# Moving sums of the first product into DRAM transfers, regrouping its border rounds and reordering the DFT's first steps in a spectral-plus-MoE kernel

## The chip, the cores and the metric

The kernel runs on one NeuronCore of one Trainium2 chip. The metric is the device time of one execution in microseconds (us). Five engines work side by side, each on its own queue in order: TensorE (PE, with its weight loads PEld), VectorE (DVE), ScalarE (ACT), GpSimd (POOL) and SyncE (SP), which here only issues DMA transfers. Sixteen DMA engines move the data.

## The reference

A token mixer of two branches on the same x, 2048 tokens by 512, all in float32:

```python
a = x @ dft_hid_re.T ;  b = x @ dft_hid_im.T             # DFT along the 512
A = dft_seq_re @ a - dft_seq_im @ b                        # real part of the DFT along the 2048 tokens
gates = softmax(x @ w_gate)                                # all 8 experts are taken (K = 8)
B = sum(gates[:, e] * (silu(x @ w1[e]) @ w2[e]) for e in range(8))   # hidden size 1376 per expert
g = sigmoid((x * gate_w).sum(-1))
out = g * A + (1 - g) * B
```

## The kernel before, in words

Every float32 product is made of three matmuls on operands split in two: `mm` (L348) issues high by high (L349), high by low (L352), low by high (L353). A split is two instructions: ACT copies the operand to the rounded high part (`act`, L346), and DVE or POOL subtracts it from the operand for the low part (`vt`, L343; `pt`, L340). Block products are further cut by a Strassen-like scheme with seven (2x2 blocks) or twenty (3x2x2) products, so operands are sums of blocks, made on DVE and POOL, and results are sums of products.

The program has four stages on the one core.

1. The DFT along the tokens (from the start to about 322 us) in eight phases, the list `phases` at L740: X phases use the forms 1, 2 and 5, Y phases 6, 3, 7 and 4. Each phase runs over k = 0..7. For one k, `plan_left_x` (L473) loads the four 256-wide blocks of x (`xraw`, "xr" in the rows, 512 KB), splits blocks 0 and 1 (tile "xl" from "xr"), sums blocks 2 and 3 on DVE (`s1`, tile "xq") and splits that sum (`hi`, tile "xl" from "xq"); `plan_right` (L534) loads 512 KB of the DFT matrix ("ca") and 256 KB ("cd"), takes a difference on DVE into "cd" and splits both (tiles "c12..h", "c12..l", and "c" from "cd"). `dft` (L633) issues the 18 matmuls of one k: forms 1 and 2 first, 5 last. In the first phase k = 0 and 1 are done by `dft_0` (L619), and before it `warm` (L624) issues WARM = 10 matmuls on a constant tile. In the tile names c12003l the digits are phase and k: 00 then 3.
2. The DFT along the 512 (`plan_y`, L884), four groups, to about 409 us. Beside it the twenty forms of x (`XFORM`, L76) for the next stage are made: each is one block of x transposed, or a sum or difference of two. `raw_block` (L925) loads the raw blocks, DVE adds (L986, L989, L1014, L1017), and each form is split on ACT and DVE (L997, L1020).
3. The first product of the experts (silu(x w1)), 29 rounds ("laps"), about 27 us each, to about 1195 us. A round takes three chunks of 128 hidden rows; `chunk_rows` (L44) lists them. Each expert has ten full chunks and 96 rows over; the overs of all experts make six mixed chunks. Three chunks of one expert make a pure round; what is left makes mixed rounds. `plan_round` (L1055) plans one: sums of w1 blocks on POOL (L1097), splits on ACT and POOL (L1110, L1112), 20 products, the combining sums on DVE (L1182), silu on ACT (L1198), and a multiplication by the gate of the chunk's expert on DVE (L1208). `gate` (L1037) loads that gate row spread over 128 partitions, 256 KB, and keeps it in a buffer for a following round that uses it.
4. The second product (w2), to the end.

The order of the work: in stage 1 every step is an event with a time (`ev`, L332) and the events are sorted by it; ACT, DVE, POOL and PE keep this order, and the plain loads and stores on SP are placed by the framework. From stage 2 on, a planner (`Plan.run`, L158) simulates the engines with fixed costs, gives out buffers, and the order it finds is written out. An SP transfer waits until the eighth before it on SP has landed, since eight semaphores go round.

## Time and profile before

| what | value |
|---|---|
| device time, median of 3 runs (lowest, highest) | 2019.68 us (2019.68, 2019.91) |
| the profiled execution: its own time | 2020.08 us |
| the profiled execution: span from first to last instruction | 2018.3 us |
| busy share of PE, DVE, ACT, POOL | 99%, 82%, 51%, 43% |
| matmuls | 8836 |
| moved by DMA | 475.20 MB |

The span and the 1.8 us around it make the profiled execution's own time, 0.4 us above the median. Times in the views are counted from the start of the span. An engine's idle time costs something only where PE waits for it, since PE is busy nearly throughout.

### The profile page before, as it was taken

To read this page: it belongs to the slowest core of one execution; us is meant where nothing else is said; L and a number is where in the kernel's file an instruction comes from. 1 tells how busy PE (TensorE), PEld (TensorE's weight loads), DVE (VectorE), ACT (ScalarE), POOL (GpSimd) and SP (SyncE) were. 2 spreads that over 40 slices of the span, in tenths; PEclk is the share of its full clock that TensorE was granted. 3 is DMA by queue.
4 is the path that set the end of the run, shared out by engine and by line. 5 is a ranking of instruction groups with operands and counts; after the bars stand their busy time and mean duration, and the time that the engine had idled before them with its cause. 6 is when DMAs were issued, how large, how long until landed. Compare 5 with 4: busy or idle time off the path is not lost. (4 is left out here: it accounts for less than half of the span.)

```text
span 2018.3 us, 26838 instructions
## 1 busy us (share of the span) xinstructions
PE 2006.9 (99%) x8836; PEld 1655.3 (82%) x8836; DVE 1659.0 (82%) x1929; ACT 1030.1 (51%) x1440; POOL 861.9 (43%) x829
## 2 busy tenths in 40 slices
PE   9999999999999999999999999999999999999999
PEld 7887888888888888888878888888888888888887
DVE  8998996887878887887778786687778888899875
ACT  6544453455555555555555565544445444445442
POOL 0000000188889888889798830000002221235330
PEclk9999999999999999999999999999999999999999
DMA  8676696545565546454645599899889988999991
GB/s 317 214 254 237 221 311 214 190 148 183 175 201 172 185 157 213 166 190 166 221 152 178 178 317 368 298 333 287 268 265 286 293 269 262 279 279 331 303 291 45
DMA packets 205236, 475.20 MB, mean 235 GB/s; under 512 B 22788, under 2 KB 37508, under 8 KB 205096
## 3 DMA queue, kind: packets, MB, share of 16 engines
q1 hardware_dynamic: 192280, 450.15, 64.9%
q0 software_dynamic: 12672, 23.07, 6.9%
q8 instruction: 69, 1.13, 0.2%
q14 instruction: 71, 0.58, 0.1%
q10 hardware_dynamic: 144, 0.26, 0.1%
HBM read 366.36 MB, written 107.03 MB: 235 GB/s over the span
## 5 line engine op out<-in xcount | busy, mean ns | idle before, releaser
L1198 ACT ACTIVATE psp<-psp 128x512 f32<-128x512 f32 x280 | 160.3, 582 | 208.5 <-DVE psp L1182 141.8
L1182 DVE TENSOR_TENSOR psp<-psp,tc 128x512 f32<-128x512 f32 x79 | 55.3, 699 | 33.9 <-PE psp L353 27.9
L1260 ACT ACTIVATE tc<-psp 128x512 f32<-128x512 f32 x88 | 52.4, 597 | 42.7 <-PE psp L353 32.9
L1097 POOL TENSOR_TENSOR tc<-ras 128x256 f32<-128x256 f32 x27 | 20.0, 739 | 121.9 <-DMA ras<-w_dram 120.4
L1427 POOL DMA_DIRECT2D xfx1n<-w_dram x11 | 9.9, 963 | 132.3 <-DVE xf211n L1484 94.8
L1260 ACT ACTIVATE tg<-psp 128x512 f32<-128x512 f32 x67 | 40.0, 598 | 35.4 <-PE psp L353 27.3
L1182 DVE TENSOR_TENSOR psp<-psp,tg 128x512 f32<-128x512 f32 x52 | 36.3, 699 | 21.8 <-PE psp L353 17.8
L340 POOL TENSOR_TENSOR c73011l<-cb,c73011h 128x1024 fp32r<-128x1024 f32 x1 | 2.4, 2412 | 116.8 <-ACT c73011h L346 116.8
L1112 POOL TENSOR_TENSOR wfs1nn<-tc,wfs1nn 128x512 fp32r<-128x512 f32 x32 | 42.0, 1313 | 15.4 <-ACT wfs1nn L1110 8.9
L1208 DVE TENSOR_TENSOR tc<-psp,tc 128x512 f32<-128x512 f32 x62 | 42.5, 685 | 5.2 <-ACT psp L1198 4.2
L1097 POOL TENSOR_TENSOR tc<-tc,ras 128x256 f32<-128x256 f32 x54 | 43.1, 797 | 4.2 <-DVE xfx13n L997 1.8
L1112 POOL TENSOR_TENSOR wfs3n<-tc,wfs3n 128x512 fp32r<-128x512 f32 x29 | 38.4, 1326 | 10.9 <-ACT wfs3n L1110 10.9
L1112 POOL TENSOR_TENSOR wfs2n<-tc,wfs2n 128x512 fp32r<-128x512 f32 x29 | 39.0, 1344 | 8.2 <-ACT wfs2n L1110 8.1
L346 ACT ACTIVATE c<-cd 128x512 fp32r<-128x512 f32 x32 | 20.2, 633 | 38.7 <-DVE cd L343 38.7
L1260 ACT ACTIVATE tw<-psp 128x512 f32<-128x512 f32 x41 | 24.5, 597 | 30.3 <-PE psp L353 23.3
L1182 DVE TENSOR_TENSOR psp<-psp,tw 128x512 f32<-128x512 f32 x37 | 25.9, 699 | 16.4 <-PE psp L353 14.4
L1112 POOL TENSOR_TENSOR wfs0n<-tc,wfs0n 128x512 fp32r<-128x512 f32 x26 | 35.3, 1356 | 7.8 <-ACT wfs0n L1110 7.4
L349 PE MATMUL psp<-xfx,wfs0n 128*128 128x512 f32 x94 | 36.6, 389 | 0.0
L353 PE MATMUL psp<-xfx,wfs0n 128*128 128x512 f32 x94 | 36.6, 389 | 0.0
L340 POOL TENSOR_TENSOR c12111l<-ca,c12111h 128x1024 fp32r<-128x1024 f32 x1 | 2.6, 2602 | 78.4 <-PE u L353 78.4
L1112 POOL TENSOR_TENSOR wfs0n<-tg,wfs0n 128x512 fp32r<-128x512 f32 x24 | 32.1, 1339 | 7.4 <-ACT wfs0n L1110 7.4
L1112 POOL TENSOR_TENSOR wfs3n<-tg,wfs3n 128x512 fp32r<-128x512 f32 x24 | 33.0, 1373 | 3.4 <-ACT wfs3n L1110 3.3
(3474 smaller groups left out, 7980.9 us busy)
## 6 DMA issues: line engine op xcount, KB each, us to landing
hd<-tc SPq DMA_DIRECT2D x161, 256.0 KB, 2.3
ca<-cT_dram SPq DMA_DIRECT2D x63, 512.0 KB, 5.4
hd<-tg SPq DMA_DIRECT2D x108, 256.0 KB, 2.5
hd<-tw SPq DMA_DIRECT2D x75, 256.0 KB, 2.3
cb<-cT_dram SPq DMA_DIRECT2D x32, 512.0 KB, 5.3
ras<-w_dram SPq DMA_DIRECT2D x29, 512.0 KB, 4.2
xfx12n<-hd SPq DMA_DIRECT2D x27, 512.0 KB, 5.3
ras1n<-hd SPq DMA_DIRECT2D x26, 512.0 KB, 5.4
```

The source lines that it names most:

```text
L340: pin(nc.gpsimd.tensor_tensor(*a))
L346: pin(nc.scalar.activation(dst, src, f, **kw))
L349: ins = nc.tensor.matmul(ps, lh, rh, start=start, stop=False, skip_group_check=True)
L353: nc.tensor.matmul(ps, ll, rh, start=False, stop=stop, skip_group_check=True)
L1097: pin(ins.tensor_tensor(low(b, j), src(x), src(y), o))
L1112: lambda: pin(nc.gpsimd.tensor_tensor(r(w)[:, 1, :], f(b), f(w)[:, 0, :], sub)), [oh] + deps, [b, w],
L1182: q = op("DVE", V, due, lambda: pin(nc.vector.tensor_tensor(f(dst), f(a[0]), f(b_[0]), o)), [a[1], b_[1]] + list(deps), [dst, a[0], b_[0]] ...
L1198: os = op("ACT", A, due, lambda: pin(nc.scalar.activation(f(dst), f(src_), AF.Silu, scale=sign)), [o0], [dst, src_])
L1208: oh = op("DVE", V, due + 1.2, lambda: pin(nc.vector.tensor_tensor(f(hb), f(dst), f(gb), OP.mult)), [os, og], [hb, dst, gb], lock=dst.ring ...
L1260: o = op("ACT", AP_, after(x), lambda: pin(nc.scalar.activation(f(b), f(bank[x[0]]), AF.Copy)), [prod[x]], [b, bank[x[0]]])
L1427: return op("POOL", 0.9, due, lambda: pin(nc.gpsimd.dma_start(f(src_)[:, j, :], block(key), accum_op=add, max_dma_last_dim=4096)), deps, [ ...
```

## The change

- The first matmuls: WARM goes from 10 to 17.
- The first phase of the DFT: for k = 4..7 the sum of blocks 2 and 3 of x is no longer made on DVE from the loaded x. SP loads block 2 a second time into a tile of its own, and a DMA issued by POOL adds block 3 onto it in SBUF. And for every k from 2 on (before: k = 2 alone) the low part "c12..l" is placed at s - 3.4, ahead of the difference "cd".
- The forms of x: twelve sums of two blocks, named xa to xl, are made in DRAM: SP copies one block to a DRAM tile `xs`, and a DMA issued by POOL adds the other. They are scheduled in the fourth phase of the DFT. Twelve forms are then one raw block; where the sum carries a minus sign, the sign is put into the split (ACT's scale, and a scalar_tensor_tensor on DVE). Five forms stay differences on DVE, and some forms change sign, with add and subtract exchanged in the sums of w1 blocks and the sign of one silu.
- The rounds: the mixed rounds take one mixed chunk and the last full chunk of two neighbouring experts, and stand between these two, after rounds 3, 9, 15 and 21 of the pure ones, instead of three leftover chunks in a row of the list after every second expert. The number of rounds and of products is the same.

```diff
-WARM = 10
+WARM = 17
...
-    pure = [[tuple(e * FULL + 3 * i + j for j in range(3)) for i in range(FULL // 3)] for e in range(E)]
-    rest = [e * FULL + FULL - 1 for e in range(E)] + list(range(E * FULL, NCHUNK))
-    mixed = [tuple(rest[3 * i:3 * i + 3]) for i in range(len(rest) // 3)]
     out = []
     for e in range(E):
-        out += pure[e]
-        if e % 2:
-            out.append(mixed[e // 2])
-    return out + [tuple(rest[-2:])]
+        out += [tuple(e * FULL + 3 * i + j for j in range(3)) for i in range(FULL // 3)]
+        if e % 2 == 0:
+            out.append((E * FULL + e // 2, e * FULL + FULL - 1, (e + 1) * FULL + FULL - 1))
+    return out + [(NCHUNK - 2, NCHUNK - 1)]
...
+XFORM = {16: "-21", 6: "+xa", 7: "+13", 13: "+14", 9: "+22-13", 3: "+22", 0: "+21-14", 10: "+xb",
...
+XSUM_AT = (13.0, 8.0)
...
+        def plus(j):
+            if j == 2:
+                v["q"] = xp.tile([P, 256], F32, tag="x", name=f"xq{k}_0")
+                nc.sync.dma_start(v["q"], x[k][:, j, :])
+            else:
+                pin(nc.gpsimd.dma_start(v["q"], x[k][:, j, :], accum_op=add, max_dma_last_dim=4096))
...
-        ev(s5 - 3.3, s1)
+        if k < 4:
+            ev(s5 - 3.3, s1)
+        else:
+            ev(s - 12.5, plus, 2)
+            ev(s - 8.5, plus, 3)
...
+    def x_sum(n, k, blk):
+        d, t = int(blk[0]) - 1, int(blk[1]) - 1
+        src_ = xT[2 * d:2 * d + 2, :, t * GT:(t + 1) * GT]
+        if k == 0:
+            nc.sync.dma_start(xs[n], src_)
+        else:
+            pin(nc.gpsimd.dma_start(xs[n], src_, accum_op=add, max_dma_last_dim=4096))
...
-                plan_right(pr, c, ph, k, s - 14, s - 2.9, r, lo=s - 3.4 if k == 2 else None)
+                plan_right(pr, c, ph, k, s - 14, s - 2.9, r, lo=s - 3.4)
...
+        if (pr, c, ph) == (0, 1, "Y"):
+            for n, blocks in enumerate(XSUM.values()):
+                for k, blk in enumerate(blocks):
+                    ev(T + XSUM_AT[0] * n + XSUM_AT[1] * k, x_sum, n, k, blk)
...
+    def second(dst, src, hi, neg):
+
+        if neg:
+            return nc.vector.scalar_tensor_tensor(dst, src, -1.0, hi, OP.mult, sub)
+        return nc.vector.tensor_tensor(dst, src, hi, sub)
```

The order of three queues at the places that matter. SP in the first phase, before: the loads of x ("xr") and of the DFT matrix for k = 5, 6, 7 (the digit after xr, the last digit after ca00 and cd00).

```order
L542 DMA ca005_249<-cT_dram 128x1024
L544 DMA cd005_251<-cT_dram 128x512
L481 DMA xr5_246<-x_dram 128x1024
L542 DMA ca006_288<-cT_dram 128x1024
L481 DMA xr6_285<-x_dram 128x1024
L544 DMA cd006_290<-cT_dram 128x512
L542 DMA ca007_328<-cT_dram 128x1024
L481 DMA xr7_325<-x_dram 128x1024
L544 DMA cd007_330<-cT_dram 128x512
```

SP at the same place, changed:

```order
L557 DMA ca005_259<-cT_dram 128x1024
L501 DMA xq4_0_230<-x_dram 128x256
L559 DMA cd005_261<-cT_dram 128x512
L485 DMA xr5_256<-x_dram 128x1024
L501 DMA xq5_0_272<-x_dram 128x256
L557 DMA ca006_301<-cT_dram 128x1024
L485 DMA xr6_298<-x_dram 128x1024
L559 DMA cd006_303<-cT_dram 128x512
L501 DMA xq6_0_313<-x_dram 128x256
L557 DMA ca007_342<-cT_dram 128x1024
L485 DMA xr7_339<-x_dram 128x1024
L559 DMA cd007_344<-cT_dram 128x512
```

Four loads of 128 KB ("xq") have come in between; the fourth, xq7_0, stands right behind the last row shown. DVE at the end of the first phase, before ("c12010l" is the first low part that the second phase needs, "c5007" and "xl5_6" from "xq7" are the parts of form 5 at k = 7):

```order
L343 TENSOR_TENSOR c12007l_408<-ca007_328,c12007h_407 128x1024
L343 TENSOR_TENSOR cd010_367<-cd010_367,ca010_365 128x512
L343 TENSOR_TENSOR c12010l_416<-ca010_365,c12010h_415 128x1024
L343 TENSOR_TENSOR c5007_418<-cd007_330,c5007_418 128x512
L343 TENSOR_TENSOR xl5_6_375<-xq7_0_410,xl5_6_375 128x256
```

DVE there, changed:

```order
L347 TENSOR_TENSOR c12007l_422<-ca007_342,c12007h_421 128x1024
L347 TENSOR_TENSOR cd007_344<-cd007_344,ca007_342 128x512
L347 TENSOR_TENSOR c5007_430<-cd007_344,c5007_430 128x512
L347 TENSOR_TENSOR cd010_382<-cd010_382,ca010_380 128x512
L347 TENSOR_TENSOR c12010l_428<-ca010_380,c12010h_427 128x1024
L347 TENSOR_TENSOR xl5_6_390<-xq7_0_353,xl5_6_390 128x256
```

The difference cd007 now follows c12007l, and c5007 stands ahead of c12010l. ACT's order is as before in this phase: high part of the sum xq7, then c12010h, then c5007. POOL from its start to the sixth phase, changed; before, the rows of L503 and L761 are not there:

```order
L643 MEMSET one_92 128x128
L503 DMA xq4_0_230<-x_dram 128x256
L503 DMA xq5_0_272<-x_dram 128x256
L503 DMA xq6_0_313<-x_dram 128x256
L503 DMA xq7_0_353<-x_dram 128x256
L344 ISA
L344 TENSOR_TENSOR c73011l_1135<-cb011_1088,c73011h_1134 128x1024
L344 TENSOR_TENSOR c64011l_1141<-ca011_1086,c64011h_1140 128x1024
L761 DMA xs_83<-xT_dram 256x512 x3
L344 TENSOR_TENSOR c12101l_1475<-ca101_1435,c12101h_1474 128x1024
L344 TENSOR_TENSOR c5101_1484<-cd101_1437,c5101_1484 128x512
L761 DMA xs_83<-xT_dram 256x512 x7
```

POOL holds its adding transfers in its own order: three stand behind the low part c64011l of the fourth phase and seven behind c5101 of the fifth.

More of the change, by code (lines that the diff above doesn't have):

```diff
@@ L991, in fnet_moe_kernel @@
+                dep.append(op("DVE", V2 if k is None else V, xdue[m] - 2.6, go,
                               oa + ob, [s_, a_, b_], lock=True, rel=xdue[m] - XDUE[5]))
-        last = None
+        last, neg = None, sa == "-"
         for k, (s_,) in each((src,)):
-            oh = op("ACT", A2 if k is None else A, xdue[m] - 1.4, lambda h=h, s_=s_, k=k: pin(
-                nc.scalar.activation(r(h) if k is None else r(h)[:, k, :], part(s_, k), AF.Copy)),
+            oh = op("ACT", A2 if k is None else A, xdue[m] - 1.4, lambda h=h, s_=s_, k=k, neg=neg: pin(
+                nc.scalar.activation(r(h) if k is None else r(h)[:, k, :], part(s_, k), AF.Copy, scale=-1.0 if neg else 1.0)),
@@ L996, in fnet_moe_kernel @@
                 dep, [h, s_], rel=xdue[m] - XDUE[5])
-            last = op("DVE", V2 if k is None else V, xdue[m], lambda l=l, h=h, s_=s_, k=k: pin(nc.vector.tensor_tensor(
-                r(l) if k is None else r(l)[:, k, :], part(s_, k), part(h, k), sub)), [oh, last], [l, h, s_], lock=True)
+            last = op("DVE", V2 if k is None else V, xdue[m], lambda l=l, h=h, s_=s_, k=k, neg=neg: pin(second(
+                r(l) if k is None else r(l)[:, k, :], part(s_, k), part(h, k), neg)), [oh, last], [l, h, s_], lock=True)
@@ L1011, in x_half @@
-        (qa, oa), (qb, ob) = halves
-        if sa == "-":
-            def go():
-                pin(nc.vector.scalar_tensor_tensor(f(qa), f(qa), -1.0, f(qb), OP.mult, sub))
-        else:
-            def go():
-                pin(nc.vector.tensor_tensor(f(qa), f(qa), f(qb), add if sb == "+" else sub))
-        os = op("DVE", V + 0.2 * (sa == "-"), xdue[m] - 2.6, go, [oa, ob], [qa, qb], lock=True)
-        oh = op("ACT", A, xdue[m] - 1.4, lambda: pin(nc.scalar.activation(r(h)[:, k, :], f(qa), AF.Copy)), [os], [h, qa])
@@ L1020, in x_half @@
-        return op("DVE", V, xdue[m], lambda: pin(nc.vector.tensor_tensor(r(l)[:, k, :], f(qa), f(h)[:, k, :], sub)), [oh],
+            halves.append((q, load(xdue[m] - 6, lambda q=q, blk=blk: nc.sync.dma_start(f(q), x_block(blk)[k]), MB, bufs=[q],
+                                   rel=xdue[m] - 10)))
+        qa, os = halves[0]
+        if len(terms) == 2:
+            (_, oa), (qb, ob) = halves
+            os = op("DVE", V, xdue[m] - 2.6, lambda: pin(nc.vector.tensor_tensor(f(qa), f(qa), f(qb), sub)), [oa, ob],
+                    [qa, qb], lock=True)
@@ L1021, in x_half @@
+        neg = terms[0][0] == "-"
+        oh = op("ACT", A, xdue[m] - 1.4, lambda: pin(nc.scalar.activation(
+            r(h)[:, k, :], f(qa), AF.Copy, scale=-1.0 if neg else 1.0)), [os], [h, qa])
+        return op("DVE", V, xdue[m], lambda: pin(second(r(l)[:, k, :], f(qa), f(h)[:, k, :], neg)), [oh],
                   [l, h, qa], lock=True)
@@ L1134, in plan_round @@
             s5 = sums(b5, [(1, "12", "22", add)], d4 - 4.0, [])
-            s4 = sums(b4, [(0, (b5, 1), "11", add)], d4 - 3.2, s5)
+            s4 = sums(b4, [(0, "11", (b5, 1), sub)], d4 - 3.2, s5)
             split(b4, (0, (10, 14)), d4, s4 + [u4])
@@ L1140, in plan_round @@
             u6 = unit(b6, 0, "21", d6)
-            s6 = sums(b6, [(1, "11", "32", sub)], d6 - 3.2, [])
+            s6 = sums(b6, [(1, "11", "32", add)], d6 - 3.2, [])
             split(b6, ((17, 12), 18), d6, s6 + [u6])
@@ L1144, in plan_round @@
             s7 = sums(b7, [(0, "12", "32", add), (1, "21", "31", add)], d7 - 4.2, [])
[L1145 removed]
+            s9 = sums(b9, [(1, (b7, 1), "12", sub), (1, (b9, 1), "22", sub)], d7 - 2.6, s7)
             split(b7, (15, 1), d7, s7 + s9)
@@ L1195, in finish_out @@
             row, j = divmod(i, 4)
+            sign = -sign if j == 1 else sign
             src_, o0 = val[name]
```

47 lines of the change are left out of this document (22 added, 25 removed).

## The prediction

> **What bounds the kernel now.** I read the page first, then the busy times in stretches of 50 us, then what PE waited for, then the stretches with the time line. The page's first part:
>
> ```profile
> PE 2006.9 (99%) x8836; PEld 1655.3 (82%) x8836; DVE 1659.0 (82%) x1929; ACT 1030.1 (51%) x1440; POOL 861.9 (43%) x829
> ```
>
> The matmuls stay the same 8836 but for seven more warming calls, so only PE's losses can be won. Busy time, with the number of instructions in brackets, by stretch:
>
> ```profile
> core 0: us, PE busy (x) PEld busy (x) DVE busy (x) ACT busy (x) POOL busy (x), PEclk, DMA share, GB/s
> 0.00:50.00 50.00, 46.45 (x199) 38.45 (x200) 41.84 (x69) 32.57 (x51) 0.56 (x6) 0.97 0.85 316
> 50.00:100.00 50.00, 50.00 (x222) 41.40 (x222) 49.43 (x75) 26.66 (x35) 0.00 (x0) 1.00 0.60 215
> 100.00:150.00 50.00, 49.60 (x220) 40.79 (x219) 47.91 (x62) 21.23 (x21) 4.78 (x2) 1.00 0.77 253
> ...
> 400.00:450.00 50.00, 48.97 (x216) 40.15 (x215) 41.50 (x52) 28.39 (x49) 41.02 (x37) 1.00 0.48 160
> ...
> 750.00:800.00 50.00, 49.44 (x217) 40.35 (x217) 39.76 (x57) 28.37 (x51) 42.38 (x44) 1.00 0.59 200
> ...
> 1000.00:1050.00 50.00, 48.93 (x215) 39.72 (x214) 40.16 (x56) 26.97 (x49) 43.35 (x44) 1.00 0.52 173
> ```
>
> A full stretch holds 222 matmuls, so one takes 50 / 222 = 0.225 us. The three stretches of the first product lack 6 + 5 + 7 = 18 matmuls: 18 x 0.225 = 4.1 us. The stretch from 100 lacks two, 0.5 us. The rest of the loss is in the first 50 us. What PE waited for:
>
> ```profile
> PE u L619 <- ACT c L346: 2.1, 1, 2.1
> ...
> PE psp L349 <- ACT tc L1260: 1.0, 1, 1.0
> PE psp L353 <- POOL wfs2n L1112: 0.7, 1, 0.7
> PE psp L349 <- ACT tg L1260: 0.6, 1, 0.6
> PE u L349 <- DVE s L343: 0.4, 1, 0.4
> PE psp L349 <- ACT tw L1260: 0.4, 1, 0.4
> PE u L352 <- DVE c12003l L343: 0.3, 1, 0.3
> ```
>
> So everything that this change could remove is about 4.1 us in the first product and some 2 to 3 us at the start. A gain or a loss of 0.2% is 4.0 us, about what a measurement of this kernel can tell from no change.
>
> **The change, part by part: the warming.** The start, by the clock that PE was granted (third number from the end):
>
> ```profile
> 4.07:7.49 3.42, 1.29 (x10) 1.06 (x9) 0.87 (x2) 1.53 (x3) 0.00 (x0) 1.00 0.95 354
> 7.49:10.90 3.41, 3.41 (x9) 2.64 (x8) 3.04 (x6) 1.82 (x4) 0.00 (x0) 0.50 1.04 395
> 14.30:36.00 21.70, 21.43 (x95) 17.41 (x95) 20.94 (x35) 14.91 (x24) 0.00 (x0) 1.00 1.03 403
> ```
>
> And the time line there (start, duration; the bracket is the idle time and its releaser):
>
> ```profile
> 1.15 3.88 PE L631 MATMUL warm<-one 128*128 128x128 f32 x20 [1.15 <-POOL one L628]
> 7.16 10.07 PE L619 MATMUL u<-c,xl 128*128 128x512 f32 x36 [2.13 <-ACT c L346]
> 15.12 1.23 DVE L343 TENSOR_TENSOR c12002l<-ca,c12002h 128x1024 fp32r<-128x1024 f32 x1
> 17.30 0.39 PE L352 MATMUL u<-c12002l,xl 128*128 128x512 f32 x1
> 20.53 1.22 DVE L343 TENSOR_TENSOR c12003l<-ca,c12003h 128x1024 fp32r<-128x1024 f32 x1
> ```
>
> PE was busy 1.29 of 3.42 us, and in the next 3.41 us it had half its clock. The 36 first matmuls took 10.07 us instead of 36 x 0.225 = 8.1: 1.9 us. The 20 warming matmuls (two for a call) took 3.88 us, so 14 more take 14 x 0.19 = 2.7 at most, ending at 7.7 instead of 5.03; at the full clock about half of that, so they end near 6.4, ahead of 7.16. I take full clock from then on; the ends are 0.5 us later and 1.9 us earlier. But c12002l is done at 15.12 + 1.23 = 16.35 and was used at 17.30, so at most 0.95 us of it is won before DVE is late. c12003l goes ahead of two DVE steps and keeps about that for k = 3. With DVE waiting for ACT's part of cd right behind, I carry 0.8 us into k = 4.
>
> **The sum on DMA, k = 4 to 7.** It takes 0.43 us of DVE away four times, for which PE did not wait. It adds a load of 128 KB and an adding transfer behind it. What waits for the adding transfer is ACT's high part (xl from xq), and behind that, in ACT's order, everything for the next k. The end of the first phase before:
>
> ```profile
> 22.51 0.33 SPq L544 DMA_DIRECT2D cd<-cT_dram  x1
> ...
> 34.04 0.43 DVE L343 TENSOR_TENSOR xq<-xr 128x256 f32<-128x256 f32 x1
> ...
> 34.50 0.42 ACT L346 ACTIVATE xl<-xq 128x256 fp32r<-128x256 f32 x1 [0.82 <-DVE xq L343]
> 34.82 1.05 ACT L346 ACTIVATE c12010h<-ca 128x1024 fp32r<-128x1024 f32 x1
> ...
> 35.78 0.61 ACT L346 ACTIVATE c<-cd 128x512 fp32r<-128x512 f32 x1
> 36.11 0.70 DVE L343 TENSOR_TENSOR cd<-cd,ca 128x512 f32<-128x512 f32 x1
> 36.71 1.23 DVE L343 TENSOR_TENSOR c12010l<-ca,c12010h 128x1024 fp32r<-128x1024 f32 x1
> ...
> 42.34 0.39 PE L352 MATMUL u<-c12010l,xl 128*128 128x512 f32 x1
> ```
>
> The transfers: one load alone in its window, and of the adding ones that the second product has, the whole queue and the fastest and the slowest kind (KB, then the median time to landing):
>
> ```profile
> cd<-cT_dram SPq DMA_DIRECT2D x1, 256.0 KB, 9.5
> q0 software_dynamic: 12672, 23.07, 6.9%
> xfx1n<-w_dram POOLq DMA_DIRECT2D x11, 256.0 KB, 7.5
> ...
> wfs3nn<-w_dram POOLq DMA_DIRECT2D x3, 256.0 KB, 5.2
> ```
>
> The DMA engines are full from 7.49 to 36 us (share 1.03, 403 GB/s), so every byte put in moves what follows. cd for k = 7, the last load ahead of xq7, landed at 22.51 + 9.5 = 32.0. The four xq loads add 4 x 131 KB / 403 GB/s = 1.3 us. An adding transfer of 256 KB held all engines for 0.069 x 2018.3 / 88 = 1.58 us (88 = 23.07 MB by 256 KB), so one of 128 KB holds them for 0.8, and three lie ahead: 2.4 us. xq7 lands near 35.7. The adding transfer then takes between 5.2 - 0.8 = 4.4 and 7.5 - 0.8 = 6.7 us; the engines are fuller here than there but the transfer is small, so I take 5.0, and down to 3.6 if its latency shrinks with its size. The sum lands at 40.7, where ACT had it at 34.50.
>
> From there in the changed order: ACT's parts of xq7, c12010h and c5007 start 0.32 and 0.96 us apart and the last takes 0.61, with its wait 2.0 us; then on DVE c5007 and cd010, 0.6 us each from start to start like cd above, and c12010l 1.23: about 4.5 us. c12010l is ready at 45.2 and was used at 42.34: **+2.9 us**. The ends: landing of xq7 0.7 earlier with 3.6 gives 35.0 + 3.6 + 4.5 - 42.3 = +0.8; 0.5 later with 6.7 gives +5.1. It swallows what the warming won, since PE waits here for a landing. The same chain at k = 4 (xq4 follows the load of ca for k = 5) is late by less, so the last one counts. Nothing behind gives it back: PE runs at its own pace to 400 us.
>
> The Trainium skill, page "DMA: Bandwidth & Descriptors", section "Anatomy of one DMA — SWDGE (gpsimd) path", gives such a transfer 2.0 us plus its bytes at 436 GB/s: an estimate of 2.3 us for 128 KB, by which this term would be +0.2. The rows above, 5.2 to 7.5 us for 256 KB against its 2.6, speak against that in a loaded kernel.
>
> **The sums in DRAM.** Twelve copies and twelve adding transfers of 512 KB, spread by SP's order over about 40 to 260 us. An adding one holds the engines for 3.2 us, a copy 1.5 (450.15 MB in 64.9% of the span):
>
> ```profile
> q1 hardware_dynamic: 192280, 450.15, 64.9%
> ```
>
> That is 12 x 4.7 = 56 us in 220 us, of which the shares of 0.60 to 0.77 leave 50 to 88 us free. Three adding ones stand in a row on POOL behind c64011l, in the stretch from 100 us, and seven behind c5101; each waits for its copy, and c12101l and c12111l are queued behind them, but the copies stand far ahead on SP. In the waits above PE waits for no load. I take 0, and up to +1.5 if a pile-up there outlasts the loads' lead. On the other side DVE loses some fifteen additions between 330 and 430 us, and eight low parts become scalar_tensor_tensor, which costs no more (min/median/max in ns):
>
> ```profile
> L986 DVE SCALAR_TENSOR_TENSOR xf201n<-wfs,xfw x1: 1221/1221/1221, 357.4 to 357.4; 128x1024 f32<-128x1024 f32 x1
> L989 DVE TENSOR_TENSOR wfs<-xfx,wfs x1: 1220/1220/1220, 359.6 to 359.6; 128x1024 f32<-128x1024 f32 x1
> ```
>
> DVE is busy 41.50 of 50 us there, and PE's one wait in that stretch, 1.0 us, was for ACT: I take 0, and at best that wait with its refilling, -1.3.
>
> **The rounds.** Gate loads fall by twelve of 256 KB in SP's order; every mixed round still needs three gates at once, two of which its neighbours use as well. The wait in the stretch from 750 us stands at the first product of round 14, right behind the mixed round 13 (counted from 0):
>
> ```profile
> 791.19 0.50 PE L349 MATMUL psp<-xf16n,wfs0n 128*128 128x512 f32 x1 [0.56 <-ACT tg L1260]
> ```
>
> The two of the stretch from 1000 us stand in round 22, a pure one behind a pure one. The new plan has another order everywhere, and such waits come from small differences between plan and chip. Of the 4.1 us I take 1.0 as won; the ends are -3.0 and +1.5. A changed sign costs nothing.
>
> **The sum.** +2.9 + 0 + 0 - 1.0 = +1.9 against the profiled execution's own 2020.08 us: 2022.0; against the median, which stands 0.4 us lower, 2019.68 + 1.9 = **2021.6 us**. That is +0.1%, no change that a measurement can tell. Its own range, with the ends added in part: -0.5 to +4.0, or 2019.2 to 2023.7.
>
> **The rivals.**
> Faster: the adding transfers hide. For it speaks the skill's 2.3 us; against it the rows. Then the start wins 0.8 and the laps 1.0: 2017.9 us. Below -4 us it gets only if also nearly all laps' waits go: -0.8 - 3.6 gives 2015.3.
> Slower: the landings come late and the clock closes as well. Once an adding transfer takes more than about 6.5 us, the chain costs 5 us, and PE idles 1 to 2 us within some 3.4 us, as it did before 7.49, after which it had half its clock for 3.41 us; while PE waits anyway, about 1 of those 1.7 us counts. +5.0 + 1.0 - 0.5 gives 2025.2. Against it: 1.3 to 2 us of idle are fewer than the 2.13 of the start. The skill's page "TensorE: Matmul & The Clock Gate", section "Part 1: The HAM clock gate", has the gate close after one idle window of about 3.4 us; the trace shows the half clock after a window 38% busy.
> Worse laps: the new order brings more waits than it takes, 3 us, beside +2.9: 2025.6 us.
>
> **How the numbers follow.** The forecast has 0.58, nearly all of it within 0.2%, 0.04 slower. The hidden transfers have 0.20, of which 0.08 is faster by over 0.2%. Late landings have 0.15 and worse laps 0.07, nearly all slower by over 0.2%, 0.20 together. So faster 0.08, same 0.68, slower 0.24. The range runs from 2016.8, leaving out the best of the laps, to 2025.2.
>
> **What would show it.** In the changed profile: the 36 first matmuls in about 8.2 us with the clock at 1.00; ACT waiting for a DMA ahead of xl from xq four times, near 28, 32, 36 and 40 us; the first low product of phase two near 45 us instead of 42.34; DFT stretches from 50 to 320 us full with 222; fewer than 18 matmuls missing in the first product. If xl from xq does not wait, or phase two starts before 42 us, the step on the adding transfer is wrong. If the 50 us stretches of the DFT lack matmuls, the step on the DRAM sums is.

## The result, and the profile after

| | time, us | against before |
|---|---|---|
| before | 2019.80 (2019.68 to 2020.24) | |
| changed | 2043.47 (2040.53 to 2047.44, four runs) | ratio 1.0118, 95% interval 1.0103 to 1.0133 |

The change costs 23.7 us. The forecast was +1.9, with a range that ended at 2025.2. The changed kernel also scatters more, 7 us over its four runs, where the kernel before stays within 0.6. Its profiled execution took 2047.44 us with a span of 2045.7. That is the slowest of the four, 4.0 us above their median, so the losses read from its trace are larger than the 23.7 by about as much.

The first part of its page, and the queue on which the adding transfers of POOL run (packets, MB, share of the engines):

```profile
PE 2018.8 (99%) x8850; PEld 1660.5 (81%) x8850; DVE 1643.1 (80%) x1907; ACT 1027.8 (50%) x1439; POOL 877.7 (43%) x845
...
q0 software_dynamic: 16512, 29.89, 9.0%
```

DVE did become less busy, by 16 us, and no time was won with it. The stretches of 50 us show where the matmuls are missing (a full one holds 222):

```profile
0.00:50.00 50.00, 45.23 (x190) 36.96 (x191) 34.11 (x54) 28.05 (x45) 4.18 (x10) 0.97 0.82 294
...
100.00:150.00 50.00, 48.09 (x206) 39.32 (x205) 47.50 (x63) 21.09 (x22) 6.63 (x5) 0.97 0.79 241
150.00:200.00 50.00, 46.34 (x197) 36.27 (x196) 38.86 (x47) 19.35 (x23) 7.36 (x6) 0.97 0.92 292
...
250.00:300.00 50.00, 41.84 (x178) 34.14 (x177) 34.81 (x45) 17.95 (x27) 8.63 (x9) 0.93 0.88 275
300.00:350.00 50.00, 48.96 (x212) 39.28 (x211) 46.89 (x57) 26.01 (x29) 0.00 (x0) 1.00 0.75 256
```

Everything is lost in the DFT. Stretches of the DFT that lack matmuls were the prediction's sign that its step on the DRAM sums is wrong; those from 150 us on show it. (What is missing between 100 and 150 us lies around a wait for DVE at 125.79 us and belongs to the start.) What PE waited for, the four longest:

```profile
PE u L356 <- DVE c12116l L347: 8.2, 1, 8.2
PE u L353 <- ACT c L350: 2.7, 1, 2.7
PE lt L401 <- ACT xs_2h L350: 2.5, 1, 2.5
PE u L353 <- DVE s L347: 1.9, 1, 1.9
```

In the first three the engines named, DVE and ACT, were not the cause: they waited for a transfer themselves (ahead of the third, ACT stood 7.33 us for a load "ca"). In the fourth, DVE was busy: 3.36 of the 3.43 us around it. The second wait, on the time line, with POOL's adding transfer for k = 4, ACT behind it, and PE:

```profile
22.99 1.01 POOL L503 DMA_DIRECT2D xq<-x_dram  x1 [21.89 <-DMA xq<-x_dram]
...
29.73 0.42 ACT L350 ACTIVATE xl<-xq 128x256 fp32r<-128x256 f32 x1 [5.89 <-DMA xq<-x_dram]
30.05 0.61 ACT L350 ACTIVATE c<-cd 128x512 fp32r<-128x512 f32 x1
...
30.71 0.50 PE L353 MATMUL u<-c,xl 128*128 128x512 f32 x1 [2.70 <-ACT c L350]
```

The sum for k = 4 landed 6.7 us after POOL had issued it, and ACT stood for 5.89 us. The longest wait, near 290 us:

```profile
281.15 1.60 SPq L559 DMA_DIRECT2D cd<-cT_dram  x2
...
285.26 0.39 PE L353 MATMUL u<-c12116h,xl 128*128 128x512 f32 x1
291.33 0.69 DVE L347 TENSOR_TENSOR cd<-cd,ca 128x512 f32<-128x512 f32 x1 [12.32 <-DMA cd<-cT_dram]
...
293.81 0.79 PE L356 MATMUL u<-c12116l,xl 128*128 128x512 f32 x1 [8.16 <-DVE c12116l L347]
```

SP issued the load of cd116 (the "cd" of the seventh phase at k = 6) at 281.15 us and it came 10 us later. DVE could not begin the difference before, and the low part c12116l stands behind that difference. The order of SP says why the load was issued so late. Before:

```
L542 DMA ca113_2168<-cT_dram 128x1024
L544 DMA cd116_2287<-cT_dram 128x512
L542 DMA ca114_2206<-cT_dram 128x1024
```

On the time line before, SP issued it at 233.28 us, 22.7 us ahead of ca116. In the changed kernel cd116 stands behind ca116 and seven more transfers: ca117, four stores of ud and two loads of wd. The framework has placed the loads anew; run 7 below shows that the copies on SP alone do not bring cd116 there.

The clock paid again behind these waits. The granted clock (third number from the end) in a window of 3.4 us around the wait near 193 us, and in the next one:

```profile
191.70:195.09 3.39, 1.08 (x4) 0.50 (x5) 2.73 (x4) 2.19 (x3) 0.00 (x0) 1.00 1.09 305
195.09:198.50 3.41, 3.41 (x9) 2.63 (x8) 3.27 (x5) 0.76 (x2) 0.00 (x0) 0.50 1.07 339
```

PE was busy a third of the first window and got half its clock in the second, with 9 matmuls instead of 15. Six matmuls are 6 x 0.225 = 1.4 us beside the wait itself. It happened four times in the DFT.

To follow a loss through the program I compare when the first matmul of a step starts in two time lines. The row "before" has its start in us; every other row has how much later that kernel is there. Each row is one execution; those of the changed kernel and of run 14 stand 4.0 us above and 3.8 us below the median of their runs, the others within 3 us of it. The steps are k = 5 of the first phase (c12005), the first one of the second and of the fourth phase (c12010, c64010), k = 4 of the fifth (c12104), k = 7 of the seventh (c12117), k = 1 of the eighth (c64111), the first product, and the last matmul.

| kernel | c12005 | c12010 | c64010 | c12104 | c12117 | c64111 | first product | end |
|---|---|---|---|---|---|---|---|---|
| before | 29.9 | 42.1 | 118.8 | 182.5 | 274.6 | 284.1 | 409.2 | 2013.1 |
| changed | 3.9 | 5.2 | 7.0 | 12.7 | 24.9 | 27.2 | 28.4 | 27.7 |
| 1 neither | -0.7 | 3.2 | 4.2 | 4.2 | 4.2 | 4.2 | 5.1 | 7.2 |
| 2 start adds | 3.5 | 5.1 | 6.7 | 6.7 | 6.7 | 6.7 | 6.7 | 6.8 |
| 3 DRAM sums | -0.5 | 2.8 | 4.9 | 13.2 | 28.5 | 30.6 | 31.9 | 31.2 |
| 4 copies on POOL | -0.8 | 2.7 | 4.1 | 5.0 | 23.6 | 25.2 | 27.0 | 26.9 |
| 5 low order | -0.5 | 2.7 | 4.4 | 4.4 | 4.4 | 4.4 | 4.4 | 3.9 |
| 6 warming, rounds | -0.1 | -0.1 | -0.1 | 0.0 | 0.0 | 0.0 | 0.0 | 2.4 |
| 7 no DRAM adds | -0.6 | 2.7 | 5.0 | 6.8 | 6.8 | 8.7 | 10.0 | 9.4 |
| 8 cd order | -0.5 | 2.8 | 4.8 | 12.1 | 17.1 | 24.6 | 25.8 | 26.9 |
| 9 plain | -0.5 | 2.8 | 4.8 | 8.2 | 16.6 | 18.9 | 20.4 | 20.6 |
| 10 moved | -0.7 | 2.6 | 4.6 | 7.5 | 11.2 | 15.1 | 22.0 | 21.4 |
| 11 adds, old order | 4.2 | 5.9 | 5.9 | 5.9 | 5.9 | 5.9 | 5.9 | 5.7 |
| 12 one add | 0.0 | 2.1 | 3.8 | 5.4 | 5.4 | 5.4 | 5.4 | 5.4 |
| 13 sums, no low order | 0.1 | 0.1 | 2.4 | 7.3 | 17.0 | 18.5 | 19.7 | 19.9 |
| 14 changed, no low order | 3.7 | 4.8 | 5.6 | 9.5 | 18.5 | 20.4 | 21.6 | 19.8 |
| 15 changed, cd order | 4.1 | 5.1 | 7.0 | 11.4 | 12.4 | 15.9 | 17.1 | 15.9 |

Two losses stand out in the row of the changed kernel: 7 us up to the fourth phase, and 20 more between the fourth and the eighth, where the transfers of the DRAM sums run. The experiments take the two apart. Each loss in us below is the run's median less that of the kernel before on the same chip.

### The profile page after: what moved, and what is told of

It reads as the page before. It is cut to its first block, busy times and chain, and to the rows that moved or that the text cites. A ratio compares the mean times of both kernels' runs of the same rounds, so it can differ in the third digit from the quotient of the medians.

```text
span 2045.7 us, 26911 instructions
## 1 busy us (share of the span) xinstructions
PE 2018.8 (99%) x8850; PEld 1660.5 (81%) x8850; DVE 1643.1 (80%) x1907; ACT 1027.8 (50%) x1439; POOL 877.7 (43%) x845
## 4 chain that ended last, share of the span: by engine, by line
PE 85%; DMA 4%; DVE 3%; issue 1%; POOL 1%; SPq 0%; ACT 0%; DVEq 0%; ACTq 0%; POOLq 0%
PE psp L353 27%; PE psp L356 26%; PE psp L357 26%; PE u L356 2%; PE u L353 2%; PE u L357 2%; DMA ca<-cT_dram 1%; DMA cb<-cT_dram 1%; DMA cd<-cT_dram 0%; DMA ud<-c 0%; DMA hd<-tc 0%; DVE ca L347 0%; DMA xfx11n<-hd 0%; DVE c L347 0%; DMA hd<-tw 0%
## 5 line engine op out<-in xcount | busy, mean ns | idle before, releaser
L1214 DVE TENSOR_TENSOR psp<-psp,tc 128x512 f32<-128x512 f32 x67 | 46.8, 699 | 29.1 <-PE psp L357 24.6
L761 POOL DMA_DIRECT2D xs<-xT_dram x12 | 10.8, 896 | 99.9 <-DMA xs<-xT_dram 54.5
L1144 POOL TENSOR_TENSOR wfs2nn<-tc,wfs2nn 128x512 fp32r<-128x512 f32 x36 | 48.7, 1353 | 10.0 <-ACT wfs2nn L1142 10.0
L356 PE MATMUL psp<-xfx,wfs0nn 128*128 128x512 f32 x134 | 52.1, 389 | 0.0
L356 PE MATMUL psp<-xfx,wfs3nn 128*128 128x512 f32 x132 | 51.4, 389 | 0.0
L356 PE MATMUL psp<-xfx,wfs1nn 128*128 128x512 f32 x128 | 49.8, 389 | 0.0
L356 PE MATMUL psp<-xfx,wfs2nn 128*128 128x512 f32 x126 | 49.0, 389 | 0.0
L1129 POOL TENSOR_TENSOR tc<-ras,tc 128x256 f32<-128x256 f32 x48 | 41.4, 871 | 10.1 <-issue 5.3
L1144 POOL TENSOR_TENSOR wfs3nn<-tc,wfs3nn 128x512 fp32r<-128x512 f32 x28 | 37.5, 1339 | 16.9 <-ACT wfs3nn L1142 16.7
L1129 POOL TENSOR_TENSOR tg<-ras,tc 128x256 f32<-128x256 f32 x44 | 42.7, 976 | 0.5
L347 DVE TENSOR_TENSOR cd<-cd,ca 128x512 f32<-128x512 f32 x32 | 26.3, 823 | 20.1 <-DMA cd<-cT_dram 14.9
L1241 DVE TENSOR_TENSOR tg<-psp,tc 128x512 f32<-128x512 f32 x48 | 32.9, 686 | 9.5 <-ACT psp L1231 8.9
```

The costliest lines, as they stand in the source:

```text
L347: pin(nc.vector.tensor_tensor(*a))
L356: nc.tensor.matmul(ps, lh, rl, start=False, stop=False, skip_group_check=True)
L761: pin(nc.gpsimd.dma_start(xs[n], src_, accum_op=add, max_dma_last_dim=4096))
L1129: pin(ins.tensor_tensor(low(b, j), src(x), src(y), o))
L1144: lambda: pin(nc.gpsimd.tensor_tensor(r(w)[:, 1, :], f(b), f(w)[:, 0, :], sub)), [oh] + deps, [b, w],
L1214: q = op("DVE", V, due, lambda: pin(nc.vector.tensor_tensor(f(dst), f(a[0]), f(b_[0]), o)), [a[1], b_[1]] + list(deps), [dst, a[0], b_[0]] ...
```

## The experiments: the start

**1. Neither kind of adding transfer.** The changed kernel without `plus` and without the sums in DRAM, all forms of x being made as before; warming, low order and rounds stay.

```diff
-        if k < 4:
-            ev(s5 - 3.3, s1)
-        else:
-            ev(s - 12.5, plus, 2)
-            ev(s - 8.5, plus, 3)
+        ev(s5 - 3.3, s1)
...
-            for n, blocks in enumerate(XSUM.values()):
-                for k, blk in enumerate(blocks):
-                    ev(T + XSUM_AT[0] * n + XSUM_AT[1] * k, x_sum, n, k, blk)
```

> Neither the sums in DRAM nor the adding transfers of the first phase; the warming, the order of the low parts and the regrouped rounds stay. Theory (the two kinds of transfer carry the whole loss, and the rest is a small gain): 0.9 us won at the start, as PE stood 0.86 us earlier at c12002h in the changed trace, and about 1.8 us in the first product, which took 783.6 us instead of 785.4; so 2016 to 2018.5 us, no stall over 1 us in the DFT. Rival (the new order of the rounds or of the low parts has a loss of its own that the others hide): 2020 us or more, with stalls in the DFT or the first product that the kernel before does not have.

Measured: 2026.82 us, ratio 1.0034 (1.0020 to 1.0047), +7.05. The theory fell: without a single adding transfer the kernel is still slower than before. By the table 4.2 us are lost up to the fourth phase, which run 5 follows; the 3 us behind the DFT were not taken apart.

**2. The first phase's adding transfers.** Run 1 with `plus`.

> The first run of this series plus the adding transfers of the first phase (k = 4 to 7), still no sums in DRAM. Theory (the first of these transfers is late by its whole 6.7 us, ACT and behind it DVE stand still, and DVE, full until the fourth phase, never makes it up): PE 4 to 5 us later from k = 5 on, about 7 us at the first product of the fourth phase (c64010h), one or two more half clocks of 1.7 us, and nothing given back; 7 to 9 us above the first run of this series, 2024 to 2027 us. Rival (what I predicted: the delay at the last k counts alone, and PE's slack up to the fourth phase takes up the rest): 2 to 4 us above the first run.

Measured: 2027.45 us, 1.0039 (1.0024 to 1.0054), +7.7. That is only 0.6 above run 1, less than either theory had. PE is indeed late at k = 5 and 6.7 us late at c64010, but run 1 loses most of that without them.

**5. The low order alone.** The kernel before with one line changed.

```diff
-plan_right(pr, c, ph, k, s - 14, s - 2.9, r, lo=s - 3.4 if k == 2 else None)
+plan_right(pr, c, ph, k, s - 14, s - 2.9, r, lo=s - 3.4)
```

> The kernel before with one edit: the low part of c12 at s - 3.4 for every k from 2 on in the first phase. Theory (in the first run the low part no longer covers ACT's split of cd: DVE waits 0.78 us for ACT in every k and needs 4.49 us for a k, where it needed 3.62 us before and PE needs 4.08): DVE falls behind PE over five k, PE stands still for about 2 us at the end of the first phase (the low part of the last xq), half a clock window follows, and the 4 us are never made up: 2023.3 to 2025 us. Rival (the first run lost its time by the regrouped rounds or by an accident of its plan): within 1 us of the kernel before.

Measured: 2025.46 us, 1.0026 (1.0016 to 1.0037), +5.3. The theory stands. DVE over one k, first before and then in run 5:

```profile
26.82 0.42 DVE L343 TENSOR_TENSOR xq<-xr 128x256 f32<-128x256 f32 x1
27.15 0.69 DVE L343 TENSOR_TENSOR cd<-cd,ca 128x512 f32<-128x512 f32 x1
27.75 1.23 DVE L343 TENSOR_TENSOR c12005l<-ca,c12005h 128x1024 fp32r<-128x1024 f32 x1
28.89 0.69 DVE L343 TENSOR_TENSOR c<-cd,c 128x512 fp32r<-128x512 f32 x1
...
31.36 1.23 DVE L343 TENSOR_TENSOR c12006l<-ca,c12006h 128x1024 fp32r<-128x1024 f32 x1
```

```profile
28.54 1.22 DVE L343 TENSOR_TENSOR c12005l<-ca,c12005h 128x1024 fp32r<-128x1024 f32 x1
29.67 0.41 DVE L343 TENSOR_TENSOR xq<-xr 128x256 f32<-128x256 f32 x1
30.01 0.68 DVE L343 TENSOR_TENSOR cd<-cd,ca 128x512 f32<-128x512 f32 x1
31.47 0.69 DVE L343 TENSOR_TENSOR c<-cd,c 128x512 fp32r<-128x512 f32 x1 [0.78 <-ACT c L346]
...
33.02 1.22 DVE L343 TENSOR_TENSOR c12006l<-ca,c12006h 128x1024 fp32r<-128x1024 f32 x1
```

Before, the low part stands between cd and c, and ACT makes its copy of cd in that time. With the low part moved ahead, DVE stands 0.78 us in every k. From one low part to the next it needs 33.02 - 28.54 = 4.48 us where it needed 31.36 - 27.75 = 3.61. PE needs 4.08 for a k (before, the first matmul of k = 4 starts at 25.79 and that of k = 5 at 29.87), so DVE, which was ahead of PE, falls behind. At the end of the phase PE waits for it, and since DVE is 99% busy up to the fourth phase, it never catches up.

**6. Warming and rounds alone.** The kernel before with `WARM = 17` and the new `chunk_rows`.

> The kernel before with the 17 warming calls and the regrouped rounds alone. Theory (DVE is the engine that sets the first half of the DFT, so what the warming wins at the start is waited for again at the first product of the fourth phase, where PE waited for DVE already; the rounds trade about 0.7 us less in the first product for 1 to 1.8 us more at the start of the second): 2019 to 2021 us, no change that can be measured. Rival (the warming's 0.9 us stay, and the rounds win what the changed trace showed, 1.8 us): 2017 to 2018 us.

Measured: 2020.55 us, 1.0002 (0.9993 to 1.0012). The 1.0 us that the warming wins is gone at c12004 of the first phase, and the rounds win nothing that can be measured (the 2.4 us at the end of its row in the table belong to one execution; the median is +0.4).

**11. The first phase's adding transfers alone.** The kernel before with `plus` for k = 4 to 7, and **12.** for k = 7 alone (`if k < 7`).

> The kernel before with the adding transfers of the first phase for k = 4 to 7 and nothing else; the low parts stay where they were. Theory (the first adding transfer is late by itself: its load lands at 22.7 us, it takes 6.7 us, and ACT would have had the sum at about 23.5 us): ACT waits some 5 to 6 us once, PE is 4 to 6 us late at c12005 and 5 to 7 us at c64010h: 2024 to 2027 us. Rival (the second run stood only 0.6 us above the first, so the adding transfers are nearly free and the late low part is the whole loss of the start): 2020 to 2022 us.

Measured: 2025.10 us, 1.0025 (1.0015 to 1.0034), +5.1.

> As the run before, with one adding transfer, for k = 7 alone. Theory (any first one is late by its own landing time, and the others are late by little because everything behind the first is already late): ACT waits 3 to 6 us for it and PE is 3 to 5 us late from the second phase on: 2022.5 to 2025 us. Rival (each k pays its own share, 1.1 to 1.2 us as for k = 5, 6 and 7 in the changed trace): 2020 to 2021.5 us.

Measured: 2024.72 us, 1.0024 (1.0015 to 1.0033), +4.75. What ACT waited for ahead of the first sum in run 11, and ahead of the only one in run 12:

```profile
30.05 0.42 ACT L346 ACTIVATE xl<-xq 128x256 fp32r<-128x256 f32 x1 [7.33 <-DMA xq<-x_dram]
```

```profile
39.61 0.42 ACT L346 ACTIVATE xl<-xq 128x256 fp32r<-128x256 f32 x1 [5.99 <-DMA xq<-x_dram]
```

Both theories held in time (in run 12 PE was 2.1 us late at the second phase, where 3 to 5 were expected, and 3.8 at the fourth): ACT waits 6 to 7 us for the first sum wherever it stands, and the ones behind it are nearly free, since everything is late already. Runs 1, 2, 5, 11 and 12 all lie between +4.75 and +7.7 and don't add up. I read this from the table: each of these edits makes PE 3.8 to 6.7 us late at c64010, where it waits for DVE, and two edits together hold DVE up over the same time.

## The experiments: the sums in DRAM

**3. The sums alone.** The changed kernel without `plus`.

> The changed kernel without the adding transfers of the first phase: the sums in DRAM alone beside the warming, the low parts and the rounds. Theory (they cost by themselves what the trace shows behind the fourth phase, from 8.6 us late at c64011h to 27.2 us late at c64111h): 15 to 20 us above the first run, 2032 to 2037 us, with PE standing still for several us in the two X phases of the second half, near 190 and 290 us. Rival (the loads were only late there because the start had used up the lead): under 8 us above the first run.

Measured: 2050.04 us, 1.0153 (1.0138 to 1.0168), +30.3, and 23.2 above run 1. That is more than the theory had and more than the whole changed kernel.

**4. The copies on POOL.**

```diff
-            nc.sync.dma_start(xs[n], src_)
+            pin(nc.gpsimd.dma_start(xs[n], src_))
```

> As the run before, with the twelve copies issued by POOL too, next to their adding transfers. The bytes are the same, but SP's queue holds no copy, and the order of its loads is nearly that of the first run up to 250 us. Theory S (the loss comes from SP's queue: the copies stand among the loads and hold its eight semaphores, and loads were moved behind stores): within 0 to 5 us of the first run, 2016 to 2023 us. Theory D (the loss comes from the time that the transfers take on the DMA engines, whoever issues them): within 4 us of the run before, 2030 to 2040 us, with the DMA engines full and loads landing 9 us and more behind their issue near 190 and 290 us. POOL waiting for a copy ahead of its low parts (c12101l, c12111l) would be a third cause, seen as PE or DVE waiting for POOL.

Measured: 2046.93 us, 1.0132 (1.0115 to 1.0149), 3.1 less than run 3. That is Theory D by its distance to run 3, though not by its 2030 to 2040 us, which run 3 itself had missed. SP's queue being free of copies saves 3 us at most.

**7. Without the twelve adding transfers.**

```diff
-            pin(nc.gpsimd.dma_start(xs[n], src_, accum_op=add, max_dma_last_dim=4096))
+            return
```

> The third run (the sums in DRAM without the first phase's adding transfers) with the twelve adding transfers left out, so that the forms are single blocks instead of sums; the twelve copies on SP and everything behind stay. Theory D (the adding transfers hold the DMA engines, 9 us each and one behind the other from 127 to 294 us, and the loads beside them land late): most of the third run's 23 us above the first go, 2027 to 2033 us, and the loads of the two X phases of the second half land 5 to 8 us after issue again. Theory S (SP's queue, with the copies in it and another order of the loads): within 6 us of the third run, 2044 us or more.

Measured: 2028.25 us, 1.0042 (1.0027 to 1.0057), +8.1, and 1.1 above run 1: the copies alone cost about 1 us, and Theory D holds. Without the adding transfers 22.2 of run 3's +30.3 are gone. But the edit changes a second thing. In run 7 SP issues ca116 and cd116 one right behind the other:

```profile
263.28 1.42 SPq L553 DMA_DIRECT2D ca<-cT_dram  x1
264.75 0.81 SPq L555 DMA_DIRECT2D cd<-cT_dram  x1
```

In run 3 ca116 is issued at 277.53 us and cd116 at 284.49, with ca117 and others between them, as in the changed kernel. So the 22.2 us hold the place of cd116 as well, which run 8 takes apart.

**9. Plain copies in their place.**

```diff
-            pin(nc.gpsimd.dma_start(xs[n], src_, accum_op=add, max_dma_last_dim=4096))
+            pin(nc.gpsimd.dma_start(xs[n], src_))
```

> The third run with each of the twelve adding transfers made a plain copy of the same 512 KB, issued by POOL at the same place (the forms are then the second block alone instead of the sum). Theory A (the loss goes with the time that the transfers hold the DMA engines: 3.2 us for an adding one, 1.5 us for a copy, by the queues' rows of the kernel before): of the 21.8 us that the adding transfers cost, about half stays, 2036 to 2041 us. Theory B (it is the adding, not the bytes: a plain transfer passes between the loads): 2028 to 2032 us, as without them. Theory C (POOL's queue, which waits for each copy, or the order): 2046 us or more.

Measured: 2038.04 us, 1.0087 (1.0070 to 1.0104), +18.1. The time is that of Theory A, but cd116 stands late here too (273.96 us, behind ca116 at 266.67), and PE's longest wait is the one for it:

```profile
PE u L356 <- DVE c12116l L347: 4.7, 1, 4.7
```

From 125 to 300 us, the queues (share of the 16 engines) and the median landing of the loads, in the kernel before:

```profile
q1 hardware_dynamic: 17019, 45.30, 76.5%
...
ca<-cT_dram SPq DMA_DIRECT2D x34, 512.0 KB, 5.3
...
cd<-cT_dram SPq DMA_DIRECT2D x11, 256.0 KB, 6.9
```

in the changed one:

```profile
q1 hardware_dynamic: 16928, 43.00, 68.2%
q0 software_dynamic: 3264, 6.29, 22.6%
...
ca<-cT_dram SPq DMA_DIRECT2D x30, 512.0 KB, 8.1
...
xs<-xT_dram POOLq DMA_DIRECT2D x12, 512.0 KB, 9.6
xs<-xT_dram SPq DMA_DIRECT2D x8, 512.0 KB, 8.7
...
cd<-cT_dram SPq DMA_DIRECT2D x14, 256.0 KB, 10.0
```

and in run 9:

```profile
q0 software_dynamic: 1728, 6.29, 12.4%
...
ca<-cT_dram SPq DMA_DIRECT2D x32, 512.0 KB, 6.5
...
cd<-cT_dram SPq DMA_DIRECT2D x11, 256.0 KB, 8.6
```

The same 6.29 MB hold the engines for 0.226 x 175 = 39.6 us as adding transfers and for 0.124 x 175 = 21.7 us as copies. (The edit also drops the option `max_dma_last_dim=4096`, and the copies go in 1728 packets instead of 3264; what of the difference is the adding and what the packets was not taken apart.) The median landings of ca and cd grow by 3 us beside the adding transfers and by 1.2 and 1.7 us beside the copies.

In medians run 3 loses 22.2 us more than run 7, and run 9 10.0 more. Neither is the price of the engines' time alone, since cd116 is late in both. Run 8, below, has cd116 right behind ca116 as run 7 has, and loses 16.7 us more than run 7 while its adding transfers hold the engines for 0.229 x 175 = 40.1 us: 0.4 us of PE for each microsecond of the engines. Copies with cd116 in its place were not run. So it is shown that the transfers of POOL cost this time and that the loads beside them land later, but between Theory A and Theory B, the engines' time or the adding as such, run 9 does not decide.

The busy times of that stretch, before and changed, give a loss of the same size in matmuls, 773 - 689 = 84, or 84 x 0.225 = 18.9 us:

```profile
125.00:300.00 175.00, 175.00 (x773) 141.91 (x773) 164.43 (x203) 87.95 (x105) 9.83 (x8) 1.00 0.77 260
```

```profile
125.00:300.00 175.00, 162.28 (x689) 129.72 (x690) 144.26 (x181) 74.09 (x88) 25.20 (x22) 0.96 0.91 282
```

**8. The place of cd116.** Run 3 with a few loads of SP kept in program order, so that cd116 stands right behind ca116.

```diff
+                hold = pin if (pr, c) == (1, 1) else (lambda i: None)
-                nc.sync.dma_start(v["a"], cT[c, pr, k][:, 0:2, :])
+                hold(nc.sync.dma_start(v["a"], cT[c, pr, k][:, 0:2, :]))
...
-                nc.sync.dma_start(v["d"], cT[c, pr, k][:, 2, :])
+                hold(nc.sync.dma_start(v["d"], cT[c, pr, k][:, 2, :]))
...
-            nc.sync.dma_start(v["t"], wd[c, d2:d2 + 2].rearrange("d p e -> p d e"))
+            pin(nc.sync.dma_start(v["t"], wd[c, d2:d2 + 2].rearrange("d p e -> p d e")))
```

> The third run with the loads of the phase (1,1,X) and those of wd kept in the order of the program on SP: cd116 stands behind ca116 again, not behind ca117, four stores and three loads of wd. No byte is moved more or less. Theory O (in the third run PE stood 8.9 us near 297 us because cd116 was issued so late, and the half clock of 10 us around it is its consequence): the step of 10.6 us between c12107 and c12117 falls to under 3 us, and the run to 2039 to 2043 us. Theory D (the DMA engines are full there, and whatever is asked for lands late): the wait moves to another load of that phase and the time stays within 4 us of the third run's 2050.

Measured: 2044.96 us, 1.0120 (1.0105 to 1.0135), some 5 us less than run 3 and between the ranges of the two theories. Both have a part: in the traces the loss up to c12117 falls by 11.4 us, but 7.5 of it come back by c64111, where run 3 loses 2.1. The longest wait of PE is now this one:

```profile
PE u L353 <- ACT c64110h L350: 3.1, 1, 3.1
```

**15. The same edit on the changed kernel.**

> The changed kernel with the loads of the phase (1,1,X) and of wd kept in program order on SP, as in the eighth run. Theory O (cd116's place behind ca117, four stores and three loads of wd makes PE's longest wait of 8.2 us, of which about half comes back one phase later): the wait on c12116l goes, the time falls by 3 to 6 us, 2037 to 2041 us. Rival (with the engines full the place in the queue decides nothing): 2042 us or more.

Measured: 2038.41 us, 1.0094 (1.0075 to 1.0114), 5.1 less than the changed kernel. Theory O, though the four runs (2033.94 to 2041.88) overlap a little with those of the changed kernel.

**10. The sums moved into the gaps.** Run 8 with the copies issued by ACT at times of their own.

```diff
-XSUM_AT = (13.0, 8.0)
+XSUM_AT = (56, 62, 69, 91, 113, 119, 155, 161, 190, 239, 245, 303)
...
-            nc.sync.dma_start(xs[n], src_)
+            pin(nc.scalar.dma_start(xs[n], src_))
...
-                    ev(T + XSUM_AT[0] * n + XSUM_AT[1] * k, x_sum, n, k, blk)
+                    ev(XSUM_AT[n] + 7 * k, x_sum, n, k, blk)
```

> As the run with the order of cd116 mended (the eighth), with the twelve copies issued by ACT at times of their own, the adding transfers behind them on POOL: copies at 56, 62, 69, 91, 113, 119, 155, 161, 190, 239, 245 and 303 us of the plan, chosen where the DMA share of the kernel before is low (0.23 to 0.62 in stretches of 6 us), not every 13 us from 117 on. Theory P (it matters where they run: beside loads that already fill the engines they delay the loads, in the gaps they don't): the stalls near 152, 192 and 235 us shrink to under 1 us each, 2028 to 2034 us. Theory E (each adding transfer costs about the same wherever it runs, since even a short one lets the loads beside it land late): 2040 to 2046 us, with the stalls moved to the new places.

Measured: 2041.67 us, 1.0106 (1.0091 to 1.0121). The time lies in the range of Theory E, but for another reason: from c64010 to c64111 PE now loses 10.5 us instead of 19.8, as Theory P had it in kind, but almost 7 us are lost behind, before the first product. There ACT waits for a load of the DFT's results; what that owes to the last of the sums was not taken apart.

**13 and 14. Does the start change the price of the sums?** Run 3, and the changed kernel, with the low parts at their old place (`lo=s - 3.4 if k == 2 else None`).

> The third run with the low parts at their old place: sums in DRAM beside the warming and the regrouped rounds, and a start that by the sixth run loses nothing. Theory L (a PE that starts later gives the loads beside the sums more lead, so the sums cost less the more the start has lost: 23 us on a start 4.2 us late, 16 us on one 6.7 us late): 30 us or more above the sixth run, 2048 us or more, so that mending the start wins nothing. Theory F (the sums cost about 22 us whatever the start does, and what lies between is chance in how transfers fall): 2040 to 2045 us.

Measured: 2039.16 us (2037.22 to 2044.48), 1.0099 (1.0084 to 1.0114).

> The changed kernel with the low parts at their old place. The start then loses what the adding transfers alone cost, 5.9 us instead of 6.97 at c64010h. Theory F: 1 us less than the changed kernel or the same, 2041 to 2044 us. Theory L: the same or more, by the lead that the loads lose, 2043 to 2047 us. If it falls below 2038 us, both are wrong, and the order of the low parts costs more in company than alone.

Measured: 2043.37 us, 1.0112 (1.0097 to 1.0128). Theory L falls, and Theory F holds but for 0.8 us in run 13: on a start that loses nothing the sums cost 2039.16 - 2020.55 = 18.6 us (run 13 less run 6), beside the adding transfers 2043.37 - 2025.10 = 18.3 (run 14 less run 11), and in the changed kernel 2043.47 - 2027.45 = 16.0. Only run 3 less run 1 gives more, 23.2. So the sums cost 16 to 23 us, in no order with the start, in kernels whose own runs scatter by up to 7 us. All four hold the late cd116; with it in its place the sums cost 17.8 us (run 8 less run 1, each against its own before) and 10.8 (run 15 less run 2). Which of the late landings makes run 3 the worst stays open.

No version beats the kernel before; the nearest, run 6, is the same to within what the runs can tell.

## Why the prediction was wrong, step by step

**The sums in DRAM: the step that failed.** It read: twelve copies and twelve adding transfers take 56 us of the engines in 220 us, 50 to 88 us are free, PE waits for no load, "I take 0". The price of one transfer was right (3.2 forecast, 39.6 / 12 = 3.3 measured). Three things about the comparison were not.

- The stretch was too long. The prediction saw that POOL holds its adding transfers behind c64011l, which runs at 127 us. So all twelve run from 129.6 us on, one behind the other, and with the eight copies of that stretch they ask for some 52 us of the engines (39.6 + 8 x 1.5), not in 220 but in 175 us, of which 0.235 x 175 = 41 were free.
- A free share is a mean. The loads need the engines at given times, and beside the adding transfers their median landing was 3 us later. It grows long before the mean is used up: run 9 asks for 21.7 + 7 x 1.5 = 32 us out of 41, and its ca and cd land 1.2 and 1.7 us later.
- "PE waits for no load" is true of the kernel before, and says that the loads' lead is enough there. It does not say how much lead is left over: less than the 3 us by which the landings grew, for the loads that PE came to wait for.

The pile-up was named and bounded at +1.5 us; it was 16 to 23. And the prediction did not look at where the framework would put the other loads on SP: the place of cd116 alone is 5 of these (runs 8 and 15). cd116 stands late in the changed kernel and in runs 3, 4, 9, 13 and 14, which all have the twelve transfers on POOL, and not in run 7, which has the copies alone.

**The low order.** The prediction saw that "DVE waiting for ACT's part of cd" would come right behind the moved low part, and still carried a gain of 0.8 us. It did not make the sum for one k: 0.78 us of waiting in each of five k is 4 us, on the engine that is 99% busy for the next 70 us. Alone this edit costs 5.3 us.

**The sum on DMA.** The chain at k = 7 was timed well: xq7 landed at 34.7 us (forecast 35.7), its sum at 41.5 (40.7), and c12010l was ready at 45.9 (45.2). The adding transfers took 6.7 us where the prediction took 5.0. The median of the four (KB, us to landing):

```profile
xq<-x_dram POOLq DMA_DIRECT2D x4, 128.0 KB, 6.7
```

But this chain is not what made PE late. The first low product of the second phase came at 47.53 us, 1.6 us after c12010l was ready. It is 5.2 us late, just beyond the end of +5.1, where +2.9 was forecast; that it came so near is luck. PE's only wait of more than 0.3 us behind k = 4 was a short one, for the low part of the last sum, which stands behind c12010l on DVE:

```profile
46.26 0.50 PE L357 MATMUL u<-c,xl 128*128 128x512 f32 x1 [0.57 <-DVE xl L347]
```

Most was lost at k = 4: PE was 1.0 us early at c12004 and 3.9 late at c12005, by the wait of 2.7 us and the half clock behind it. The sentence that "the same chain at k=4 is late by less, so the last one counts" was the wrong way round. ACT waits 5.89 us for the first sum and 1.1 to 1.2 for those behind it, and one sum alone costs 4.75. "Nothing behind gives it back" was right. In the changed kernel 5.2 us at c12010 even grow to 7.0 at c64010, where PE waits 1.9 us for DVE; in run 11, with the adding transfers alone, it stays at 5.9.

**The clock gate** was in the rival that ended slower, once, at one us. It closed four times. **The warming** and **the rounds** cost and bring nothing, within their ranges. The warming calls ended at 1.15 + 7.00 = 8.15 us, later than the 7.7 given as the most, but the 36 first matmuls took 8.46 us instead of 10.07 at a granted clock of 1.00, near the forecast of 8.2, and c12002 began 0.9 us earlier. **The saving on DVE** was rightly put at nothing.

Of the rivals, the slower one had the right sign and the right places at the start. Its price was 5 us, and it did not hold the sums in DRAM at all.

## What to carry to other kernels

When work moves from an engine to DMA, don't compare its time on the DMA engines with the mean free share: look where the queue that issues it will let it run, and set it against the free time of that stretch alone. Even below that, it delays the loads beside it, so compare the growth of their landing time with the lead that they have. Where a framework places the loads, read the new order of each load that an engine waits for, also far from the edit. And when an instruction is moved ahead on a busy engine, write down the cycle of one iteration with the other engine's part in it: what stood between a request and its answer was the cover for the answer.
